# A mixture-of-experts guess computed in other steps and on VectorE alone, three query turns placed between exponentials, and expert weights loaded one matrix at a time

## The chip, the cores and the metric

The kernel runs on one NeuronCore of a Trainium2 chip. The metric is the device time of one execution in microseconds (us). The median of three runs of the kernel before is 532.5 us (531.18 to 532.99). The core has a matrix engine (TensorE, PE in the profile; its weight loads are PEld), VectorE (DVE), ScalarE (ACT), GpSimd (POOL), and SyncE (SP), which here only issues DMAs. Each engine works through its own instructions in the order in which the program lists them.

## What is computed

Attention with one shared key and value head per batch entry (8 entries, 16 query heads, 384 positions, head size 64), followed by a mixture of experts over 3072 tokens of width 1024: a group is picked by argmax of four logits, then an expert by argmax of four more, and the token goes through that expert's two 1024 x 1024 matrices.

```
scores = scale * q @ k.T ;  attn = softmax(scores) ;  attn_out = attn @ v
x = attn_out transposed and reshaped to (8*384, 16*64)
g_idx = argmax(x @ w_group) ;  g_w = softmax(...)[g_idx]
for each group g, each expert e of it:
    h = max(x_tokens @ w1[g, e], 0) ;  out[tokens] = g_w * e_w * (h @ w2[g, e])
```

## The kernel before, in words

**Tiling.** A batch entry (b) has three tiles of 128 queries, so there are 24 tiles (t). A tile has 8 units of two heads by 64 queries. The program is one long list of 96 steps (the loop over `i`, line 901), two units a step: four steps make a tile, twelve a batch entry. `at(step, place, function)` puts an action at a named place of a step, and `run(i, place)` calls it there; this fixes the order of each engine's instructions when the program is written. Nothing is reordered later.

**A step** does, in program order: the score matmuls of its first unit (L206, place "u" behind them), those of its second unit (place "s"), then `soft` (L212): a row maximum on VectorE for each unit (L217) and two exponentials on ScalarE for each unit (L220), with place "b" between the two units. Then come places "m0", "m1", "m3" with pieces of the expert's matmuls (`advance`), places "p", "v" and "m2", the 32 x 32 block transposes of the units of two steps ago on VectorE into a three-part buffer called `ring` (L241), place "w", the reciprocal of the sums on VectorE (L231) and the four normalising multiplications on GpSimd (L235), and places "e", "o" and "g".

**Scores** go to one of two PSUM buffers in turn, so the scores of a unit wait until the exponentials of the unit two before have been read out. The value matmuls (L257, `pv`) of a tile run two to four steps after the tile's last scores. For the first five tiles the queries are turned on TensorE (`q_group`, L174: four transposes, L183, into PSUM, then a copy on ScalarE, L187): each tile in two halves of eight heads. The second half of tile t is turned in step 4t, or 4t+1 where t is 1, 2 or 3, and is first used by the scores of step 4t+2; the first half of tile t+1 is turned in step 4t+1 and used from step 4t+4. Later tiles are turned on VectorE (`q_blocks`, L195). The load of tile t+2's queries (`load_q`, SP) stands at place "g" of the step that turns the last of tile t, whose buffer it takes.

**The guess.** Before any token's real gate is known, the kernel guesses one expert for each batch entry, so that this expert's weights can be loaded early. It adds up all value rows (`guess_load`, a 768 KB load on SP, and `guess_sum`, four additions on GpSimd, L360 and L361), forms their mean on TensorE (`guess_mean`, L370), its gate logits on TensorE (`guess_logits`, L382), picks the expert in one-hot form with seven small operations, four on VectorE and three on GpSimd (`guess_pick`, L389 to L413), spreads the result to all partitions on TensorE (`guess_all`, L419) and turns it into index numbers (`guess_index`, one operation on GpSimd, two on VectorE). All of it uses parts of `ring` that are not needed before step 6. What guess picks wrongly is handled by a loop at the end.

**Weights.** `load_main(b, 0)` and `load_main(b, 1)` load the first and second matrix of entry b's expert, each with two DMAs of 1024 KB (as landed, in bf16) issued by GpSimd (`load_w`, L536). There are two buffers of each matrix. The expert of entry b (`main_expert`, L561 for the first matrix, L575 for the second) starts on TensorE in step 12(b+1)+5 and is spread over twelve steps; it reads the first matrix for about seven of them, then the second. The expert of entry 0 therefore starts in step 17. `scale_k` (GpSimd, L167) and `k_blocks` (VectorE, L171) prepare the next entry's keys in steps 12b+7 and 12b+8.

Of the kernel before, what the change touches and what calls it, by code (L numbers as in the profile page):

```python
# [14 lines left out]
ALU = mybir.AluOpType  # L15
# [4 lines left out]
def kernel(  # L20
# [81 lines left out]
    def load_q(t, first=False):  # L102
        b, j = t // ST, t % ST
        q_sb = qpool.tile([P, 2 * H * D], FP32, tag="q", bufs=2)
        if t < TQ:
            q_sb = q_sb[:, 0:H * D].rearrange("p (h d) -> p h d", h=H)
            qv = q[b].rearrange("h (j r n) d -> j n r h d", n=QN, r=32)
            for h0 in range(0, H, H // 2 if first else H):
                for n in range(QN):
                    (nc.scalar if first and (n == 1 if h0 == 0 else n % 2) else nc.sync).dma_start(  # L110
                        out=q_sb[32 * n:32 * (n + 1), h0:h0 + (H // 2 if first else H), :],
                        in_=qv[j, n, :, h0:h0 + (H // 2 if first else H), :],
                    )
# [233 lines left out]
    def guess_load():  # L347
        vs = ring[:, 2, 0:2].rearrange("p u h s -> p (u h s)").rearrange("p (b c d) -> p b c d", b=B, d=D)
        nc.sync.dma_start(
            out=vs.rearrange("p b c d -> p b (c d)"), in_=v.rearrange("b o (p c) d -> p (b o) (c d)", c=ST)  # L350
        )
        st["vs"] = vs
# [36 lines left out]
    def guess_pick():  # L389

        lg = st["guess"]
        mx = [early[name][0:B] for name in ("mx", "sm")]
        oh = early["oh"][0:B].rearrange("b (g e) -> b g e", e=4)
        pair = early["pair"][0:B].rearrange("b (g e) -> b g e", e=Eg)
        spread = early["spread"][0:B].rearrange("b (c e) -> b c e", e=GE)
        gp = nc.gpsimd
        nc.vector.tensor_reduce(out=mx[0], in_=lg, axis=AX.X, op=ALU.max)
        gp.tensor_tensor(out=lg, in0=lg, in1=mx[0].unsqueeze(2).to_broadcast([B, 1 + G, 4]), op=ALU.subtract)
        nc.vector.scalar_tensor_tensor(
            out=lg, in0=lg, scalar=0.0, in1=w4[0:B, 0:1 + G, :], op0=ALU.is_ge, op1=ALU.mult  # L400
        )
        nc.vector.tensor_reduce(out=mx[1], in_=lg, axis=AX.X, op=ALU.max)
        nc.vector.tensor_tensor(
            out=oh, in0=lg, in1=mx[1].unsqueeze(2).to_broadcast([B, 1 + G, 4]), op=ALU.is_equal
        )
        gp.tensor_tensor(
            out=pair, in0=oh[:, 1:1 + G, :], in1=oh[:, 0, :].unsqueeze(2).to_broadcast([B, G, Eg]), op=ALU.mult
        )
        gp.tensor_tensor(
            out=spread, in0=pair.rearrange("b g e -> b (g e)").unsqueeze(1).to_broadcast([B, B, GE]),  # L410
            in1=ident[0:B, 0:B].unsqueeze(2).to_broadcast([B, B, GE]), op=ALU.mult,
        )
        st["guess"] = spread  # L413
# [10 lines left out]
            st["ohs", b] = [ohs_all[:, ts(b, GE)]]  # L424

    def guess_index():
        nc.gpsimd.tensor_tensor(
            out=numbered, in0=ohs_all[:].rearrange("p (b e) -> p b e", e=GE),
            in1=tie16[:].unsqueeze(1).to_broadcast([P, B, GE]), op=ALU.mult,
        )  # L430
        number = early["number"]
        nc.vector.tensor_reduce(out=number, in_=numbered, axis=AX.X, op=ALU.add)
        idx = singles.tile([P, B], I32)
        nc.vector.tensor_scalar(
            out=idx[:], in0=number, scalar1=-1.0, scalar2=float(GE - 1), op0=ALU.mult, op1=ALU.add
        )
        st["idx"] = idx
# [365 lines left out]
    def at(slot, where, fn, *args):  # L803
        later.setdefault((slot, where), []).append((fn, args))
# [6 lines left out]


    for x, where, fn in (
        (2, "e", guess_sum), (3, "m2", guess_mean), (4, "m2", guess_logits), (4, "e", guess_pick),
        (5, "m2", guess_all), (5, "e", guess_index),
    ):
        at(x, where, fn)
    for b in range(B):
        s0 = SB * b
        for x, j0, j1 in ((s0 + 8, 0, 1), (s0 + 16, 1, ST)) if b == B - 1 else ((s0 + 16, 0, ST),):  # L820
            at(x, "m2", logits, b, j0, j1)
            at(x + 1, "m0" if j1 < ST else "v", logits_out, b, j0, j1)
        if b == B - 1:
            at(s0 + 9, "m0", gate_first, b)
            at(s0 + 9, "m3", gate_choose, b)
            at(s0 + 9, "w", gate_score, b)
            at(s0 + 10, "w", gate_pick_second, b)
            at(s0 + 1, "g", load_main, b, 0)
            at(s0 + 6, "g", load_main, b, 1)
            at(s0 + 11, "g", load_second, 0)  # L830
        else:
            at(s0 + (9 if b else 7), "g", load_main, b, 0)
            at(s0 + (9 if b else 7), "g", load_main, b, 1)
            at(s0 + 16, "g", keep_xb, b)
        at(s0 + 17, "v", gate_masks, b)
        x = s0 + 18
        at(x, "e", gate_values, b)
        at(s0 + (19 if b == B - 2 else 22), "w", gate_selected, b)
        if b + 1 < B:
            at(s0 + 2, "g", load_k, b + 1)  # L840
            at(s0 + 4, "g", load_v, b + 1)
            at(s0 + 7, "g", scale_k, b + 1)
            at(s0 + 8, "e", k_blocks, b + 1)
    for t in range(NT):
        spread = 0 < t <= ST
        for x, u, half in ((4 * t + spread, t, 1), (4 * t + 1, t + 1, 0)):
            if u < TQ:
                at(x, "m1", q_group, u, half)
            elif u < NT:
                at(x, "e", q_blocks, u, half)  # L850
        if t < NT - 2:
            at(4 * t + spread, "g", load_q, t + 2)
        x, n0 = 4 * t + 4, 0
        for p, where, n1 in (
            ((2, "p", 4), (3, "u", 6), (3, "p", 8), (4, "u", 10), (4, "p", NB)) if t < ST - 1 else
            ((2, "p", NB // 2), (3, "p", NB)) if t < NT - 1 else ()
        ):
            at(x + p, where, pv, t, n0, n1)
            n0 = n1
            if n1 == NB:  # L860
                at(x + p, "o", pv_out, t)

    load_k_first()
    load_q(0, first=True)
    load_q(1)


    wge = singles.tile([P, KO, 32], FP32)
# [28 lines left out]
    busy(1)  # L897
    q_group(0, 0, 2)
    load_v(0)
    guess_load()  # L900
    for i in range(NSL):
        t, p = i // 4, i % 4
        if i >= SB + 5 and (i - 5) % SB == 0:
# [162 lines left out]
```

## Time and profile before

| what | value |
|---|---|
| time of the profiled execution | 530.77 us |
| its span in the profile | 529.3 us |
| three timed runs | 532.5, 531.18, 532.99 us |
| mean granted TensorE clock | 0.966 |
| weights: DMA issues, size, median time to landing | 36 of 1024 KB, 15.2 us |
| HBM read, written | 102.30 MB, 19.40 MB |

The profile comes from one execution. A row of the timeline has the start (us from the span's start), the duration, the engine, the program line, the operation, what it writes and reads and how often; in brackets stands how long the engine had been idle before it, and behind the arrow what ended that wait. A row of a table by stage has the stretch, its length, the busy time and the number of instructions of each engine, the granted clock of TensorE (1.00 is full speed), the mean share of the DMA engines that were at work, and GB/s. TensorE's busy time counts cold matmuls at their longer duration, so a busy TensorE is not one at full speed.

### The profile page before, as it was taken

How to read it: one execution, taken by the hardware profiler on the slowest of the kernel's cores; microseconds unless marked ns; L12 is line 12 of the kernel's file. 1: busy time of each engine (PE TensorE's matmuls, PEld its weight loads, DVE VectorE, ACT ScalarE, POOL GpSimd, SP SyncE). 2: the span in 40 equal slices, each digit the busy share in tenths (PEclk: the TensorE clock that was granted, in tenths of full speed). 3: DMA queues.
4: the chain of work that ended last, by engine and by line, in shares of the span. 5: the costliest groups of instructions: out<-in, count | busy, mean ns of one | idle time of the engine just before them, and what ended most of it. 6: DMA issues, size and time to landing. Idle time of an engine off the chain costs nothing.

```text
span 529.3 us, 19245 instructions
## 1 busy us (share of the span) xinstructions
PE 496.1 (94%) x7868; PEld 264.3 (50%) x7868; DVE 405.0 (77%) x678; ACT 322.6 (61%) x1005; POOL 293.5 (55%) x532
## 2 busy tenths in 40 slices
PE   6569569999999999999999999999999999999994
PEld 3224225555545545554555554554555455555653
DVE  3558686998879887898789887898699888890540
ACT  4445464677666675667667666667667776663421
POOL 2744663578447655576537844765547663754300
PEclk9868798999999999999999999999999999999998
DMA  7720992638983899649982899379973999629953
GB/s 115 166 42 2 189 210 62 160 66 159 235 243 73 150 224 239 159 78 207 259 225 57 159 229 259 72 137 218 231 185 74 200 238 279 125 50 180 220 121 108
DMA packets 65561, 84.78 MB, mean 160 GB/s; under 512 B 20395, under 2 KB 41003, under 8 KB 65472
## 3 DMA queue, kind: packets, MB, share of 16 engines
q0 software_dynamic: 19152, 37.84, 39.7%
q1 hardware_dynamic: 45360, 45.40, 34.4%
q8 instruction: 63, 1.03, 0.8%
q10 hardware_dynamic: 960, 0.30, 0.2%
q14 instruction: 26, 0.21, 0.1%
HBM read 102.30 MB, written 19.40 MB: 230 GB/s over the span
## 4 chain that ended last, share of the span: by engine, by line
PE 86%; DMA 4%; DVE 3%; ACT 2%; POOL 2%; issue 1%; SPq 0%; POOLq 0%; DVEq 0%; ACTq 0%
PE x L257 24%; PE s L206 24%; PE x L561 14%; PE x L575 12%; DMA q_sb<-in_q_dram 4%; PE sb L575 4%; ACT pr L220 2%; PE sb L561 2%; PE x L280 2%; DVE nmx L217 2%; DVE ring L241 1%; POOL pr L235 1%; PE x L756 1%; PE x L100 1%; PE x L771 0%
## 5 line engine op out<-in xcount | busy, mean ns | idle before, releaser
L235 POOL TENSOR_SCALAR pr<-pr,rinv 128x384 f32<-128x384 f32 x384 | 218.3, 588 | 166.1 <-DVE rinv L231 148.6
L220 ACT ACTIVATE pr<-s,nmx 128x384 f32<-128x384 f32 x384 | 218.1, 579 | 148.1 <-DVE nmx L217 117.4
L217 DVE TENSOR_REDUCE nmx<-s 128x2 f32<-128x768 f32 x192 | 174.9, 949 | 67.9 <-PE s L206 67.1
L241 DVE STREAM_TRANSPOSE ring<-pr 128x768 f32<-128x768 f32 x192 | 175.2, 951 | 0.6 <-PE x L257 0.6
L206 PE MATMUL s<-kt,qt 64*64 64x384 f32 x1536 | 154.9, 515 | 14.2 <-ACT qt L187 8.1
L257 PE MATMUL x<-ring,v_sb 32*64 32x256 f32 x4608 | 144.7, 385 | 1.3 <-issue 1.0
L257 PEld LDWEIGHTS x<-ring,v_sb 32*64 32x64 f32 x4608 | 101.4, 133 | 53.6 <-issue 33.1
L206 PEld LDWEIGHTS s<-kt,qt 64*64 64x64 f32 x1536 | 49.7, 136 | 84.5 <-ACT pr L220 31.5
L220 ACT ACTIVATION_READ_ACCUMULATOR pr<-s,nmx 128x1 f32 x384 | 77.7, 202 | 0.0
L561 PE MATMUL x<-xb,w 128*128 128x384 bf16 x448 | 76.5, 326 | 0.0
L561 PEld LDWEIGHTS <-w 128*128 128x128 bf16 x512 | 48.1, 98 | 42.5 <-issue 12.6
L575 PE MATMUL x<-w,h_t 128*128 128x512 bf16 x288 | 65.3, 380 | 0.0
L575 PEld LDWEIGHTS <-h_t 128*128 128x128 bf16 x384 | 35.7, 98 | 52.0 <-issue 11.9
L271 ACT COPY xt<-x 128x256 f32<-128x256 f32 x96 | 29.1, 387 | 4.2 <-PE x L257 4.1
L536 POOL DMA_DIRECT2D w<-in_moe_w_dram x36 | 27.8, 779 | 3.2 <-PE sb L575 2.4
L272 POOL CAST xb<-xt 128x1024 bf16<-128x1024 f32 x24 | 24.9, 1038 | 6.0 <-ACT xt L271 6.0
L567 ACT ACTIVATE h_t<-x 128x384 bf16<-128x384 f32 x56 | 24.7, 503 | 3.8 <-PE x L561 3.8
L593 ACT ACTIVATE y<-x,gsel 128x512 f32<-128x512 f32 x36 | 25.0, 693 | 3.3 <-PE x L575 3.3
L195 DVE STREAM_TRANSPOSE qt<-q_sb 128x512 f32<-128x512 f32 x38 | 26.1, 687 | 0.0
L575 PE MATMUL sb<-w,h_t 128*128 128x512 bf16 x96 | 21.5, 379 | 0.0
L593 ACT ACTIVATE y<-sb,gsel 128x512 f32<-128x512 f32 x9 | 6.2, 687 | 16.6 <-PE sb L575 16.6
L231 DVE RECIPROCAL rinv<-ssum 128x4 f32<-128x4 f32 x96 | 13.5, 140 | 3.2 <-ACT pr L220 3.2
(154 smaller groups left out, 161.0 us busy)
## 6 DMA issues: line engine op xcount, KB each, us to landing
w<-in_moe_w_dram POOLq DMA_DIRECT2D x36, 1024.0 KB, 15.2
q_sb<-in_q_dram SPq DMA_DIRECT2D x76, 224.0 KB, 5.4
out_dram<-y SPq DMA_DIRECT2D x96, 128.0 KB, 5.9
xb_scratch<-xb SPq DMA_DIRECT2D x8, 768.0 KB, 4.5
v_sb<-in_v_dram SPq DMA_DIRECT2D x32, 96.0 KB, 3.5
kk<-in_k_dram SPq DMA_DIRECT2D x28, 92.0 KB, 4.0
q_sb<-in_q_dram SPq DMA_DIRECT2D x16, 128.0 KB, 5.2
ring<-in_v_dram SPq DMA_DIRECT2D x1, 768.0 KB, 5.8
```

Source lines behind the costliest of these rows:

```text
L195: nc.vector.transpose(out=qt[:].rearrange("p (x d) -> p x d", d=32), in_=q_sb[:, :, 0:32])
L206: nc.tensor.matmul(out=s[m * D:(m + 1) * D, h, 0:S], lhsT=qt[r, ts(2 * cc + m, D)], rhs=kt[r, :], start=True, stop=True, tile_position=(h ...
L217: nc.vector.tensor_reduce(out=nmx[:], in_=s[:, :, 0:S], axis=AX.X, op=ALU.max, negate=True)
L220: nc.scalar.activation(out=pr[:, h, :], in_=s[:, h, 0:S], func=ACTF.Exp, bias=nmx[:, h:h + 1], scale=1.0, accum_out=ssum[:, k, h:h + 1],)
L235: nc.gpsimd.tensor_scalar(out=pr, in0=pr, scalar1=rinv[:, k, h:h + 1], scalar2=1.0, op0=ALU.mult, op1=ALU.mult)
L241: nc.vector.transpose(out=ring[:, (u // 4) % 3, u % 4].rearrange("p h s -> p (h s)"), in_=st.pop(("pr", u))[:].rearrange("p h s -> p (h s)"),)
L257: nc.tensor.matmul(out=o[i][h * D:(h + 1) * D, 0:2 * P].rearrange("d (g c q) -> d g c q", g=2, c=4), lhsT=v_sb[r, n, :], rhs=ring[r, a:z + ...
L271: nc.scalar.copy(out=xt[:, :, ts(i, 32)], in_=o[:, 0:2 * P].rearrange("p (c q) -> p c q", c=KO))
L536: nc.gpsimd.dma_start(out=w[:, o:o + 4, :], in_=(w1f, w2f)[n][ds(e, 1), :, o:o + 4, :].rearrange("o p c f -> (o p) c f"))
L561: nc.tensor.matmul(out=hp[:, 0:S], lhsT=w1[:, ko, ts(fc, P)], rhs=xb[:, ko, :], start=(ko == 0), stop=(ko == KO - 1))
L575: nc.tensor.matmul(out=yp, lhsT=h_t[:, fo, ts(j, P)], rhs=w2[:, fo, ts(nh, 512)], start=(fo == 0), stop=(fo == FO - 1),)
L593: nc.scalar.activation(out=y[:, ts(nh, 512)], in_=yp, func=ACTF.Copy, scale=g)
```

## The change

Three things change.

- The load for the guess is issued on SP right behind the first two query loads, ahead of the five small loads of the gate weights and of the first values. The guess's parts move: the sum from step 2 to step 1 (place "e"), the mean from step 3 to 2 and the logits from 4 to 3 (both "m2"), the pick from place "e" of step 4 (behind the reciprocal and the multiplications) to place "w" of step 4 (ahead of them), the index from place "e" of step 5 to "w" of step 6. All operations of the pick and of the index now run on VectorE; the four additions of the sum stay on GpSimd.
- For tiles 1, 2 and 3, the second half is turned at place "b" of steps 5, 9 and 13, between the exponentials of the step's two units, and no longer at "m1" behind all four.
- The two matrices of an expert are loaded in different steps: for entry 0 in steps 10 and 15 (both in step 7 before), for entries 1 to 6 in steps 12b+7 and 12b+11 (both in 12b+9 before), for entry 7 in steps 87 and 91 (85 and 90 before).

```diff
-        gp = nc.gpsimd
         nc.vector.tensor_reduce(out=mx[0], in_=lg, axis=AX.X, op=ALU.max)
-        gp.tensor_tensor(out=lg, in0=lg, in1=mx[0].unsqueeze(2).to_broadcast([B, 1 + G, 4]), op=ALU.subtract)
+        nc.vector.tensor_tensor(out=lg, in0=lg, in1=mx[0].unsqueeze(2).to_broadcast([B, 1 + G, 4]), op=ALU.subtract)
...
-        gp.tensor_tensor(
+        nc.vector.tensor_tensor(
             out=pair, in0=oh[:, 1:1 + G, :], in1=oh[:, 0, :].unsqueeze(2).to_broadcast([B, G, Eg]), op=ALU.mult
         )
-        gp.tensor_tensor(
+        nc.vector.tensor_tensor(
             out=spread, in0=pair.rearrange("b g e -> b (g e)").unsqueeze(1).to_broadcast([B, B, GE]),
...
     def guess_index():
-        nc.gpsimd.tensor_tensor(
+        nc.vector.tensor_tensor(
             out=numbered, in0=ohs_all[:].rearrange("p (b e) -> p b e", e=GE),
...
-        (2, "e", guess_sum), (3, "m2", guess_mean), (4, "m2", guess_logits), (4, "e", guess_pick),
-        (5, "m2", guess_all), (5, "e", guess_index),
+        (1, "e", guess_sum), (2, "m2", guess_mean), (3, "m2", guess_logits), (4, "w", guess_pick),
+        (5, "m2", guess_all), (6, "w", guess_index),
...
-            at(s0 + 1, "g", load_main, b, 0)
-            at(s0 + 6, "g", load_main, b, 1)
+            at(s0 + 3, "g", load_main, b, 0)
+            at(s0 + 7, "g", load_main, b, 1)
             at(s0 + 11, "g", load_second, 0)
         else:
-            at(s0 + (9 if b else 7), "g", load_main, b, 0)
-            at(s0 + (9 if b else 7), "g", load_main, b, 1)
+            at(s0 + (7 if b else 10), "g", load_main, b, 0)
+            at(s0 + (11 if b else 15), "g", load_main, b, 1)
...
             if u < TQ:
-                at(x, "m1", q_group, u, half)
+                at(x, "b" if half and spread else "m1", q_group, u, half)
...
     load_q(1)
+    guess_load()
...
     load_v(0)
-    guess_load()
```

More of the change, by code (lines that the diff above doesn't have):

```diff
@@ L395, in guess_pick @@
         spread = early["spread"][0:B].rearrange("b (c e) -> b c e", e=GE)
-        gp = nc.gpsimd
         nc.vector.tensor_reduce(out=mx[0], in_=lg, axis=AX.X, op=ALU.max)
-        gp.tensor_tensor(out=lg, in0=lg, in1=mx[0].unsqueeze(2).to_broadcast([B, 1 + G, 4]), op=ALU.subtract)
+        nc.vector.tensor_tensor(
+            out=lg, in0=lg, in1=mx[0].unsqueeze(2).to_broadcast([B, 1 + G, 4]), op=ALU.subtract
+        )
         nc.vector.scalar_tensor_tensor(
@@ L426, in guess_index @@
     def guess_index():
-        nc.gpsimd.tensor_tensor(
+        nc.vector.tensor_tensor(
             out=numbered, in0=ohs_all[:].rearrange("p (b e) -> p b e", e=GE),
```

## The prediction

> **What bounds the kernel now.** I read the page first, then the table by stage.
>
> ```profile
> span 529.3 us, 19245 instructions
> ...
> PE 496.1 (94%) x7868; PEld 264.3 (50%) x7868; DVE 405.0 (77%) x678; ACT 322.6 (61%) x1005; POOL 293.5 (55%) x532
> ...
> PEclk9868798999999999999999999999999999999998
> ```
>
> ```profile
> 20.00:38.00 18.00, 11.11 (x98) 5.77 (x102) 9.45 (x17) 7.62 (x27) 9.65 (x18) 0.67 0.29 69
> ...
> 155.00:480.00 325.00, 324.49 (x5403) 174.34 (x5409) 278.34 (x439) 218.45 (x689) 200.24 (x354) 1.00 0.80 172
> ```
>
> From 155 to 480 us TensorE is busy for 324.49 of 325 us at clock 1.00: every wait of another engine there is covered, and only less matmul work would shorten it. Nothing in the change removes matmuls. Before about 96 us it is otherwise: TensorE has gaps and runs below full speed, at 0.67 from 20 to 38 us. So the change is worth what it does to the time at which entry 0's expert starts (step 17). The starts of the score matmuls, the rows of the first unit of steps 2 to 17, without step 12's, in order, show where that time is:
>
> ```profile
> 13.27 0.88 PE L206 MATMUL s<-kt,qt 64*64 64x384 f32 x8 [0.86 <-ACT pr L220]
> ...
> 16.72 0.88 PE L206 MATMUL s<-kt,qt 64*64 64x384 f32 x8 [1.45 <-ACT pr L220]
> ...
> 24.45 2.84 PE L206 MATMUL s<-kt,qt 64*64 64x384 f32 x16
> ...
> 28.42 2.84 PE L206 MATMUL s<-kt,qt 64*64 64x384 f32 x16 [0.50 <-ACT pr L220]
> ...
> 37.15 2.84 PE L206 MATMUL s<-kt,qt 64*64 64x384 f32 x16 [2.60 <-ACT qt L187]
> ...
> 43.44 0.88 PE L206 MATMUL s<-kt,qt 64*64 64x384 f32 x8
> ...
> 47.15 0.88 PE L206 MATMUL s<-kt,qt 64*64 64x384 f32 x8
> ...
> 51.22 0.88 PE L206 MATMUL s<-kt,qt 64*64 64x384 f32 x8 [0.29 <-ACT pr L220]
> ...
> 59.55 2.84 PE L206 MATMUL s<-kt,qt 64*64 64x384 f32 x16 [5.30 <-ACT qt L187]
> ...
> 64.89 0.88 PE L206 MATMUL s<-kt,qt 64*64 64x384 f32 x8
> ...
> 72.67 0.88 PE L206 MATMUL s<-kt,qt 64*64 64x384 f32 x8 [0.30 <-ACT pr L220]
> ...
> 80.31 2.84 PE L206 MATMUL s<-kt,qt 64*64 64x384 f32 x16
> ...
> 86.37 1.52 PE L206 MATMUL s<-kt,qt 64*64 64x384 f32 x16
> ...
> 90.60 1.52 PE L206 MATMUL s<-kt,qt 64*64 64x384 f32 x16
> ...
> 94.16 0.88 PE L206 MATMUL s<-kt,qt 64*64 64x384 f32 x8
> ```
>
> Call the distance from one step's start to the next its pitch. An undisturbed step takes 3.45 us without value matmuls (step 2), 3.71 with half a tile's share (step 7), 4.23 where a full half tile's value matmuls run (step 15). Five steps stand out: 3 (7.73), 5 (8.73), 6 (6.29), 9 (8.33) and 13 (7.64). Each of them, except step 6, leaves TensorE idle, and the next matmuls then run at half clock: sixteen score instructions take 2.84 us there and 1.52 at 86.37.
>
> **The change part by part.** The rows behind the stalls, from the timeline, and two of the page's DMA list (the load for the guess, the early query loads; the last number is the median time to landing):
>
> ```profile
> 6.24 0.42 SPq L870 DMA_DIRECT2D wge<-in_moe_w_group_dram  x1
> ...
> 14.65 2.27 POOL L235 TENSOR_SCALAR pr<-pr,rinv 128x384 f32<-128x384 f32 x4 [1.16 <-DVE rinv L231]
> ...
> 22.72 0.72 POOL L361 TENSOR_TENSOR ring<-ring 128x256 f32<-128x256 f32 x1
> ...
> 23.50 1.02 PE L370 MATMUL x<-ident,ring 128*64 128x1 f32 x16 [0.85 <-POOL ring L361]
> ...
> 30.04 0.13 DVE L397 TENSOR_REDUCE ring<-ring 8x5 f32<-8x20 f32 x1
> ...
> 32.70 0.17 DVE L399 SCALAR_TENSOR_TENSOR ring<-ring,w 8x20 f32<-8x20 f32 x1 [2.53 <-POOL ring L398]
> ...
> 33.19 1.80 DVE L217 TENSOR_REDUCE nmx<-s 128x2 f32<-128x768 f32 x2
> ...
> 35.39 0.58 ACT L220 ACTIVATE pr<-s,nmx 128x384 f32<-128x384 f32 x1
> ...
> 36.52 1.07 ACT L187 COPY qt<-x 128x512 f32<-128x512 f32 x2
> ...
> 39.66 0.29 DVE L432 TENSOR_REDUCE ring<-ring 128x8 f32<-128x128 f32 x1 [2.83 <-POOL ring L427]
> ```
>
> ```profile
> q_sb<-in_q_dram SPq DMA_DIRECT2D x16, 128.0 KB, 5.2
> ...
> ring<-in_v_dram SPq DMA_DIRECT2D x1, 768.0 KB, 5.8
> ```
>
> Sum and mean: no gain. The four additions stay on GpSimd and the mean stays one step behind them, so TensorE, which works in order, now waits ahead of step 3's scores. The value load takes the place of 6.24 on SP, so with 5.8 it lands at about 12 and is not what GpSimd waits for. Step 1's multiplications end at 14.65 + 2.27 = 16.92, four additions of 0.72 end at 19.9, and the second half of the mean's matmuls needs 1.0 more (23.44 to 24.45 today): step 3 starts at 20.9, 4.2 later than today. Step 3's own pitch falls from 7.73 to step 4's 3.97, which is also half clock: 3.8 back. Net loss 0.4. Next in line are the logits: their copy of the mean finds ScalarE empty, and the gate weights and first values, 0.4 later on SP, are needed in steps 3 and 6.
>
> Pick. VectorE today goes from 30.04 to 33.19 with the pick, 3.15 us, because its second operation waits for GpSimd's, queued behind step 4's multiplications. From 32.70 to 33.19 three of the small ones follow each other, 0.16 each; at 0.2 the seven on VectorE are 1.4: 1.75 off step 5's pitch. Bounds for the seven: 1.1 (0.16 each) and 2.0 (0.29 each, the 128 x 128 row). Queued behind it now are step 4's reciprocal and multiplications, first needed by the transposes of step 6: covered.
>
> Turn between exponentials. Step 6's scores wait for a copy (2.60 idle) that stands behind all four exponentials; the second unit's two run from 35.39 to 36.52. Moved ahead of them, the copy comes 1.13 earlier in steps 5 and 9. The added wait on ScalarE, the transposes on TensorE, is over by then (they follow the scores at once). Queued behind the copy are the second unit's exponentials, 0.6 later; the next step's second scores wait for them, which follow 0.6 behind the first anyway at full speed. I take 1.13; bounds 0 and 1.13. So step 5 becomes 8.73 - 1.75 - 1.13 = 5.85: 2.9 gained.
>
> Step 6 lost its time to half-clock score and value matmuls and to VectorE's 2.83 wait for the numbering on GpSimd. With step 5's gap down from 2.6 to about 1 us I take the pitch of step 7, 3.71: 2.6 gained. The index now costs VectorE about 0.3 + 0.29 + 0.17 (the 128 x 128 reduction's 0.29 as the nearest row for the new operation), 0.75 on step 7's start of maxima: 0.75 lost.
>
> ```profile
> 51.31 3.25 POOL L536 DMA_DIRECT2D w<-in_moe_w_dram x4
> ...
> 55.14 0.58 DVE L171 STREAM_TRANSPOSE kt<-kk 128x384 f32<-128x384 f32 x1 [2.06 <-POOL kk L167]
> ...
> 79.30 1.08 PE L183 MATMUL x<-ident,q_sb 128*128 128x128 f32 x4 [4.04 <-DMA q_sb<-in_q_dram]
> ...
> 96.09 4.07 PE L561 MATMUL x<-xb,w 128*128 128x384 bf16 x24
> ```
>
> ```profile
> 55.48 23.58 DMA q_sb<-in_q_dram
> ```
>
> Weights. Four issues hold GpSimd for 3.25 us ahead of `scale_k`, and VectorE's key transpose waits 2.06 for that in step 8. The move takes the wait out: step 9's pitch 8.33 - 2.06 - 1.13 (turn) = 5.14, 3.2 gained; step 10, at half clock today, goes from 5.34 to 3.71, 1.6 gained. The queries of tile 4 (issued at 55.48) share the DMA engines with these 4 MB and take 23.58 us; TensorE waits 4.04 for them in step 13. In the new order they go out at step 9, the first matrix one step later and behind its multiplications, so they should land in the page's 5.2, long before step 13. Step 13 becomes 3.45 + 0.6 (the copy) = 4.05, 3.6 gained; step 14, half clock today, 6.06 to 4.23, 1.8 gained. Behind the issues on GpSimd, 1.6 us in each of steps 10 and 15, stand the multiplications of steps 11 and 16, read two steps later. The later entries' moves lie under the full TensorE of 155 to 480 us: nothing; without that cover 1.6 per issue pair.
>
> Sum: -0.4 + 2.9 + 2.6 - 0.75 + 3.2 + 1.6 + 3.6 + 1.8 = 14.55. Entry 0's expert starts at 96.09 - 14.55 = 81.5. The profiled execution's own time is 530.77 (span 529.3 and 1.5 around it): 516.2. It lies 1.7 under the median of the runs, 532.5: from that, **517.9 us**, which I predict.
>
> **The rivals.** (1) The clock stays low. The stall ahead of step 3 is as long as today's ahead of step 4, so the clock should fall again. How long?
>
> ```profile
> 23.00:32.00 9.00, 8.00 (x68) 3.73 (x69) 3.77 (x6) 2.68 (x10) 4.49 (x9) 0.50 0.04 12
> ...
> 33.00:36.00 3.00, 0.63 (x3) 0.29 (x2) 2.96 (x6) 1.78 (x7) 0.60 (x2) 1.00 0.84 173
> ```
>
> For over 9 us, although TensorE was busy for 8.00 of 9. My sum has step 4 at today's half-clock pitch and full speed from step 6's value matmuls on. If it is low until their end, as until 43 us now, step 6 gains nothing (2.6) and the slow transposes and scores of step 5 eat the turn's gain there (1.1): 3.7 less, 521.6. Against it: TensorE is dense from the mean at 19.9 through step 3's scores and the logits, 4.6 us. [...]
>
> (2) The turn does not pay: the second unit's exponentials, 0.6 later, set the next step instead. For it: in step 4 one buffer's readout is what scores wait for (0.50 idle). Then 1.13 twice and 0.6 in step 13 fall away: 2.9 less, 520.8.
>
> (3) The collision moves. If the queries of tile 4 or 5 are still in flight when a matrix is issued in step 10 or 15, TensorE waits in step 13 or VectorE in step 17 as it does now: 4.04 of idle and the half clock behind it (3.6 + 1.8 of the sum at most): 523.3. Against it: step 9's issue has a whole step's lead, and one matrix is half the bytes.
>
> (4) Slower than before: the first matrix comes late. Today it is issued at 51.3 and needed at 96.1. In the new order it is issued behind step 10's multiplications, about 58, and needed at 81.5.
>
> ```profile
> DMA to landing us min/median/max: 7.9/15.2/26.6
> ```
>
> (All 36 weight issues.) At the median it is there at 75; at the worst, 85 with its second half, 4 us are lost, 521.8. Each further microsecond costs one, and from a landing at 96.1, 38 us after the issue, the kernel is slower than before; at twice the worst landing it would be there at 111, 29.5 late: 547. Nothing in the trace takes so long.
>
> (5) The change does not do what it says, in that the guess costs as much as today: then the pick and step 6 give nothing: 1.75 + 2.6 = 4.4 less, 522.3. Against: no GpSimd operation is left between VectorE's.
>
> **How the numbers follow.** Forecast 0.60, rival 1 0.14, rival 2 0.08, rival 3 0.06, rival 4 0.02 as a loss, rival 5 0.03. The remaining 0.07 is a larger gain: a stall ahead of step 3 that leaves the clock up gives 0.5 in each of steps 3 and 4, 516.9, and if the 1.7 between profile and median goes too, 515.2 and less. The range 514 to 523 takes in the bounds of pick and turn, rivals 1, 2 and 5, and leaves out rival 3, rival 4 and the far end of the larger gain, about 0.1. Faster by over 0.3% (about what a measurement of this kernel can tell from no change) 0.97, within it 0.01, slower 0.02: every rival but the fourth stays over 9 us below 532.5.
>
> **What would show it.** Right: the expert's first matmul (now L562) near 81.5 us; TensorE idle for some 3 us ahead of step 3's scores, behind GpSimd's additions; no GpSimd wait on VectorE in steps 4 to 8; steps 5, 9 and 13 with pitches of 5.9, 5.1 and 4.1; queries of tile 4 landing in under 8 us. Wrong: a wait of L562 on the weights, a DMA wait on L183, clock 0.50 beyond step 6, or any gap of TensorE after the expert's start, where my sum has none.

## The result, and the profile after

The changed kernel takes 525.56 us (median of 4 runs, 525.04 to 526.80), the kernel before 532.75 in the same session (531.18 to 534.17): a ratio of 0.9869, 95% interval 0.9835 to 0.9903. It is 7.2 us faster. The forecast was 517.9, a gain of 14.6 with a range of 514 to 523: the sign was right, half of the gain is missing, and the time lies outside the range.

The page of the changed kernel: its span, TensorE's busy time, the granted clock in 40 slices, the DMA queue that carries instructions and the later query loads (the last number is the median time to landing in us).

```profile
span 525.4 us, 19232 instructions
...
PE 495.2 (94%) x7851; PEld 264.3 (50%) x7868; DVE 405.6 (77%) x682; ACT 322.7 (61%) x1005; POOL 292.5 (56%) x528
...
PEclk9779899999999999999999999999999999999998
...
q8 instruction: 63, 1.03, 0.8%
...
q_sb<-in_q_dram SPq DMA_DIRECT2D x76, 224.0 KB, 11.3
```

The busy time of TensorE is that of before to a microsecond; the clock dips in three slices instead of five; the later queries land in 11.3 us at the median instead of 5.4. What changed is where TensorE is idle. First the front. The timeline of TensorE in the changed kernel, with the score matmuls at which steps 3, 4, 5, 6, 9, 10, 11, 13, 14 and 15 begin, and the expert's first matmul:

```profile
18.34 0.63 PE L370 MATMUL x<-ident,ring 128*64 128x1 f32 x16 [3.19 <-POOL ring L361]
...
20.78 2.83 PE L206 MATMUL s<-kt,qt 64*64 64x384 f32 x16
...
24.75 2.84 PE L206 MATMUL s<-kt,qt 64*64 64x384 f32 x16 [0.50 <-ACT pr L220]
28.71 2.84 PE L206 MATMUL s<-kt,qt 64*64 64x384 f32 x16 [1.13 <-ACT pr L220]
...
34.50 0.88 PE L206 MATMUL s<-kt,qt 64*64 64x384 f32 x8 [0.91 <-ACT qt L187]
...
46.15 0.88 PE L206 MATMUL s<-kt,qt 64*64 64x384 f32 x8
...
51.39 0.88 PE L206 MATMUL s<-kt,qt 64*64 64x384 f32 x8 [2.06 <-ACT qt L187]
...
53.36 3.57 PE L257 MATMUL x<-ring,v_sb 32*64 32x256 f32 x64
56.86 0.88 PE L206 MATMUL s<-kt,qt 64*64 64x384 f32 x8
...
64.64 0.88 PE L206 MATMUL s<-kt,qt 64*64 64x384 f32 x8 [0.30 <-ACT pr L220]
...
69.20 0.88 PE L206 MATMUL s<-kt,qt 64*64 64x384 f32 x8 [1.54 <-ACT qt L187]
...
73.92 1.52 PE L206 MATMUL s<-kt,qt 64*64 64x384 f32 x16
...
83.65 4.07 PE L562 MATMUL x<-xb,w 128*128 128x384 bf16 x24
```

The front went nearly as forecast. The wait for GpSimd's additions stands ahead of step 3 (3.19 us), step 3 starts at 20.78 (forecast 20.9), step 5's pitch is 34.50 - 28.71 = 5.79 (5.85), step 9's 5.24 (5.14), and the 4.04 us wait for tile 4's queries is gone. Entry 0's expert starts at 83.65 instead of 96.09: 12.44 us gained, where the sum had 14.55.

From there on the lead is lost again. In before 529.3 - 96.09 = 433.2 us lie between the expert's first matmul and the end, in the changed kernel 525.4 - 83.65 = 441.75. The table by stage, at the stretch that the prediction called full (the first numbers are its length and TensorE's busy time; in before the latter was 324.49):

```profile
155.00:480.00 325.00, 319.60 (x5221) 171.12 (x5241) 266.87 (x418) 211.34 (x664) 195.46 (x347) 1.00 0.79 168
```

TensorE is now idle for 5.4 us of a stretch in which the sum had nothing, at clock 1.00. The waits of TensorE from 97 to 500 us (total, times, longest), first before:

```profile
PE x L257 <- issue: 1.0, 3, 0.5
```

and after:

```profile
PE x L257 <- issue: 5.2, 8, 1.0
PE s L206 <- DVE ring L241: 0.3, 1, 0.3
```

No engine and no semaphore released these waits: "issue" is time in which the engine waited for nothing that the profile shows, and all of it stands ahead of the value matmuls. One of the eight, after, in the second half of the value matmuls of step 35:

```profile
166.12 2.88 PE L257 MATMUL x<-ring,v_sb 32*64 32x256 f32 x96
168.93 1.52 PE L206 MATMUL s<-kt,qt 64*64 64x384 f32 x16
170.38 1.94 PE L257 MATMUL x<-ring,v_sb 32*64 32x256 f32 x52
173.28 1.54 PE L257 MATMUL x<-ring,v_sb 32*64 32x256 f32 x44 [0.96 <-issue]
```

The same group in before:

```profile
181.53 2.85 PE L257 MATMUL x<-ring,v_sb 32*64 32x256 f32 x96
```

A full group of 96 takes 2.85 us. This one stops after 52 matmuls, and the pieces on both sides of the gap are long too: 4.44 us from its start to its end, 1.59 over 2.85. I call this the group's excess. Over all groups after the expert's start (those with over 0.15 us of it) it is 13.1 us in the changed kernel and 5.1 in the first profile of before; 0.5 more stand ahead of the expert there. The difference, 8.0, is most of the 8.55 lost.

### The profile page after: what moved, and what is told of

Same layout as the page of the kernel before. It is cut to its first block, busy times and chain, and to the rows that moved or that the text cites. A ratio compares the mean times of both kernels' runs of the same rounds, so it can differ in the third digit from the quotient of the medians.

```text
span 525.4 us, 19232 instructions
## 1 busy us (share of the span) xinstructions
PE 495.2 (94%) x7851; PEld 264.3 (50%) x7868; DVE 405.6 (77%) x682; ACT 322.7 (61%) x1005; POOL 292.5 (56%) x528
## 3 DMA queue, kind: packets, MB, share of 16 engines
q8 instruction: 63, 1.03, 0.8%
## 4 chain that ended last, share of the span: by engine, by line
PE 87%; DVE 4%; ACT 3%; issue 3%; POOL 2%; POOLq 0%; DVEq 0%; ACTq 0%
PE x L257 25%; PE s L206 24%; PE x L562 14%; PE x L576 12%; PE sb L576 4%; ACT pr L220 3%; PE sb L562 2%; PE x L280 2%; DVE nmx L217 2%; DVE ring L241 2%; POOL pr L235 1%; PE x L757 1%; PE x L100 1%; PE x L772 0%; PE x L183 0%
## 5 line engine op out<-in xcount | busy, mean ns | idle before, releaser
L206 PE MATMUL s<-kt,qt 64*64 64x384 f32 x1536 | 152.8, 508 | 11.3 <-ACT pr L220 6.2
L257 PE MATMUL x<-ring,v_sb 32*64 32x256 f32 x4608 | 147.7, 383 | 5.2 <-issue 5.2
L257 PEld LDWEIGHTS x<-ring,v_sb 32*64 32x64 f32 x4608 | 102.9, 132 | 57.2 <-issue 35.0
L206 PEld LDWEIGHTS s<-kt,qt 64*64 64x64 f32 x1536 | 48.5, 134 | 82.5 <-ACT pr L220 36.2
## 6 DMA issues: line engine op xcount, KB each, us to landing
q_sb<-in_q_dram SPq DMA_DIRECT2D x76, 224.0 KB, 11.3
```

The source lines that it names most:

```text
L206: nc.tensor.matmul(out=s[m * D:(m + 1) * D, h, 0:S], lhsT=qt[r, ts(2 * cc + m, D)], rhs=kt[r, :], start=True, stop=True, tile_position=(h ...
L257: nc.tensor.matmul(out=o[i][h * D:(h + 1) * D, 0:2 * P].rearrange("d (g c q) -> d g c q", g=2, c=4), lhsT=v_sb[r, n, :], rhs=ring[r, a:z + ...
```

## What stops TensorE: two theories

**Theory F (fetch).** By it, TensorE's own instructions are a transfer, and TensorE stops in the middle of a group where the next packet is late. The page has 63 packets with 1.03 MB in the instruction queue q8, 16 KB each, and TensorE ran 7868 matmuls and as many weight loads: one packet is some 250 instructions, and its loaded instructions are called a block below. A group of 96 value matmuls uses up 192 instructions in 2.85 us, sixteen score matmuls 32 in 1.52. The page counts these packets on the same 16 DMA engines as weights and queries (0.8% of their time for q8). The DMA view of the changed kernel from 168 to 176 us (40 slices of 0.2 us, the group begins at 170.38):

```profile
DMA  9999999999999999999999999999997771000000
...
q8 instruction: 2, 0.03, 1.8%
```

and of before from 176 to 184 us, ahead of the same group at 181.53:

```profile
DMA  9999995400002000694924599999999999999999
...
q8 instruction: 1, 0.02, 0.7%
```

In the changed kernel the packet starts at 170.78, amid weights and queries, and ends at 171.74; the matmuls go on at 173.28, 1.5 us after it (1.4 and 1.3 at the gaps of steps 27 and 43). In before it starts at 178.50, in the gap between two loads, 3 us ahead of its group. The times of single packets are from the trace's DMA records.

**Rival S (shift).** The later steps of the guess and the turn on ScalarE stand otherwise against the rest, and the main stage pays for that whatever the weights do.

The places of the gaps say where the boundaries are. Counted through the traces of all fourteen profiles (two instructions for a weight load and its matmul, one for every other instruction of TensorE), all 91 gaps of TensorE from 40 to 500 us that are put down to "issue", most of them in value matmuls, eight in scores, one in the expert, stand at the same place of a run of 256 instructions, the 194th or 195th. That is what a stream loaded in blocks of 256 gives, and a wait for data would not.

The packets that matter are every fifth one: the eight gaps of the changed kernel stand 1280 instructions, five blocks, or 2560 apart. Every second tile has a packet boundary inside its second half of value matmuls: steps 27, 35, 43 ... 83. For these, worked out from the trace's records: how long after TensorE began the block ahead of the missing one the packet starts (negative: earlier), and the excess of the group, in us. Here the blocks are counted as multiples of 256 from the first record; counted from the place of the gaps, all starts are 0.8 to 1.4 us larger, and the two kinds stay apart: 0.4 to 0.8 without excess, 2.4 to 3.9 with it.

```
step of the group          27    35    43    51    59    67    75    83
before         start      2.1  -0.4   1.6   2.1  -0.3   1.5   1.9  -0.1
               excess     0.8   0     0.4   0.8   0     0.6   0.8   0
after          start      2.5   3.1   3.0   2.2   2.3   2.2   2.6   3.0
               excess     1.1   1.6   1.7   1.0   0.5   1.1   1.3   1.6
```

A start of -0.4 or so goes with a DMA share of at most 0.28 in the 1.5 us ahead of it, a start of 1.5 or more with a share of 1.04 to 1.16 (packets of several queues overlap in the records, so the share can pass 1). A full share is not enough by itself: in slots_split, below, the packets of steps 27, 59 and 83 start at 0.2 to 0.7 in the table's count with a share of 1.07 to 1.12, and their groups have no excess. In before, with both matrices in one step of twelve, three of the eight packets met free engines. With the matrices in two steps, none does.

## The experiments

Twelve kernels; each ratio is to runs of the kernel before on the same chip, with its 95% interval.

**late_w_old**: the changed kernel with the old weight steps for all entries but the first.

```
-            at(s0 + (7 if b else 10), "g", load_main, b, 0)
-            at(s0 + (11 if b else 15), "g", load_main, b, 1)
+            at(s0 + (9 if b else 10), "g", load_main, b, 0)
+            at(s0 + (9 if b else 15), "g", load_main, b, 1)
```

(and 1 and 6 instead of 3 and 7 for the last entry.)

> The changed kernel with the weights of entries 1 to 7 loaded in the steps of before (both matrices in step 12b+9; 85 and 90 for the last entry); entry 0 keeps steps 10 and 15, and everything else of the change stays. Theory F (fetch): TensorE's instructions come as packets of 16 KB over the same DMA engines as the weights; with the weights spread over more of the time more of these packets start late, and TensorE stands still inside the value matmuls (the rows 'PE x L257 <- issue'). Then the issue gaps fall back to about those of before: from the expert's first matmul (83.7 us) to the end 434 us instead of 441.75, and the time is about 518.5 us (517 to 520.5). Rival S: the lead is given back because the steps of the front and the turn on ScalarE stand otherwise against the rest, whatever the weights do: it stays at 525 to 526.

521.27 us, 0.9793 (0.9757 to 0.9830): 4.3 us below the changed kernel (4.0 by the two ratios, which takes out that they ran in two sessions), with the expert's first matmul at 83.65 as there. Rival S is out. The time is 0.8 above theory F's range: the excess falls from 13.1 only to 8.1. The groups of steps 35, 59 and 83 lose theirs (packets at -0.5, -0.5 and -0.1), and the other five keep it. TensorE's row from 155 to 480 us:

```profile
155.00:480.00 325.00, 322.09 (x5314) 172.30 (x5307) 266.98 (x416) 212.63 (x668) 195.38 (x348) 1.00 0.81 173
```

**late_w_new**: the kernel before with only the later entries' weights moved, 7 and 11 for 9 and 9, and 3 and 7 for 1 and 6 in the last entry.

> The kernel before, with the weights of entries 1 to 7 alone moved to the new steps (12b+7 and 12b+11; 87 and 91 for the last); entry 0's weights, the guess and the turn stay as before. Theory F: the expert's first matmul stays at 96 us, the long groups of value matmuls (5.6 us over 2.85 each in before) add up to 12 us or so, and the time is 537 to 540 us, slower than before. Rival S (the weights' steps do not matter once TensorE is full, which is what the prediction held): 532 to 533.5.

538.01 us, 1.0104 (1.0078 to 1.0129): this part alone makes the kernel before slower by 6.2 us (531.79 there). Excess 13.5; all eight packets late (1.8 to 3.1), as in the changed kernel. The two rows, waits of TensorE from 97 to 500 us and the stretch from 155 to 480:

```profile
PE x L257 <- issue: 6.3, 9, 1.1
```

```profile
155.00:480.00 325.00, 319.74 (x5306) 171.59 (x5311) 273.03 (x432) 214.12 (x679) 193.29 (x339) 1.00 0.80 171
```

319.74 with the old front and 319.60 with the new one: the loss belongs to the weights' steps and to nothing else in the change.

**half_block**: the changed kernel with half a packet of instructions more, early.

```
+    def pad(x):
+        for _ in range(64):
+            nc.tensor.matmul(out=x[:, 0:8], lhsT=blank[:, 0:P], rhs=blank[:, 0:8], start=True, stop=True)
+    at(2, "m2", lambda: pad(xbank()))
```

> The changed kernel with 64 matmuls of 8 columns on a zero tile ahead of the guess's mean in step 2, where TensorE waits 3.19 us: 128 more TensorE instructions, half of a 16 KB packet, so that every later packet boundary falls half a packet earlier against the steps. Theory F: the long groups of value matmuls leave the second halves of the tiles at steps 27, 35, 43, 51 ... and appear, if anywhere, at those of steps 31, 39, 47 ...; the time goes anywhere from 517 to 527 as these meet the transfers or not. Rival S, or any cause in the data that the value matmuls read (VectorE's ring, the values): the same groups stay long, and the time stays within 2 us of 525.5. The clock ahead of step 3 may stay higher by these matmuls, which is read apart, from the start of the expert.

529.54 us over all nine runs (529.1 without the longest, 534.48), 0.9942 (0.9912 to 0.9972), above what either theory gave. The expert starts late, at 87.37, but not by the 64 matmuls themselves: step 15 starts at 72.23, ahead of the 73.92 of the changed kernel. Its value matmuls then stop for a packet, the longest such gap of all, and the clock is at half speed from 77.70 to 84.53:

```profile
77.89 2.82 PE L257 MATMUL x<-ring,v_sb 32*64 32x256 f32 x34 [2.23 <-issue]
```

The places are what this run was for. The changed kernel's long groups at steps 27, 35, 43, 51, 59, 67 and 83 are 2.85 us here, and long are those of 31, 39, 47, 55, 63, 71, 79 and 87 (and of 15, 19, 23 and 75). The timeline of half_block around steps 31 to 35:

```profile
151.90 2.85 PE L257 MATMUL x<-ring,v_sb 32*64 32x256 f32 x96
...
156.13 1.12 PE L257 MATMUL x<-ring,v_sb 32*64 32x256 f32 x32
158.38 1.99 PE L257 MATMUL x<-ring,v_sb 32*64 32x256 f32 x64 [1.13 <-issue]
...
171.36 2.85 PE L257 MATMUL x<-ring,v_sb 32*64 32x256 f32 x96
...
175.59 2.85 PE L257 MATMUL x<-ring,v_sb 32*64 32x256 f32 x96
```

156.13 is step 31's second half and 175.59 step 35's. Step 35 has the same data, the same weights and the same steps as in the changed kernel; the count of instructions ahead of it differs, and with it the times of the front. The gaps of over 0.15 us stand again at the 194th or 195th instruction of a run of 256, now 128 instructions earlier in the program. So what the value matmuls read is not the cause; the packet boundary is.

**no_weights**: the changed kernel without the weights of entries 2 to 7.

```
-        st.setdefault(("w", b), []).append(load_w(st["e", b], n))
+        st["last", n] = st["last", n] if b > 1 else load_w(st["e", b], n)
+        st.setdefault(("w", b), []).append(st["last", n])
```

> The changed kernel without the weight loads of entries 2 to 7 (24 of the 36 transfers of 1 MB): their experts use the matrices of entry 1, so the output differs, and the work of TensorE is the same. Theory F: with the weights off the DMA engines the instruction packets start in time, the long groups of value matmuls are left only where the loads of keys, values and queries run (13.1 us of excess in all falls to 3 to 6), and the time is 516.5 to 520. Rival S, or packets that are slow whatever the engines carry: the excess stays over 10 us and the time at 524 to 526.

517.78 us, 0.9728 (0.9702 to 0.9754), as theory F had it. That it is almost the forecast's 517.9 is in part luck: the expert starts at 83.60 here, 2.1 later than the forecast's 81.5, and the forecast had added 1.7 for the base. Excess 5.0; left are steps 19 and 27 (0.6 and 1.1, beside the weights of entry 1, still loaded), steps 43 and 67 (1.2 and 1.1, beside other loads) and one near the end (0.9). It takes the issues off GpSimd too, so by itself it does not tell these from the transfers; slots_split below keeps every issue and loses the same groups.

```profile
155.00:480.00 325.00, 322.93 (x5382) 173.94 (x5388) 268.10 (x422) 213.43 (x670) 179.00 (x326) 1.00 0.41 98
```

**slots**: weights only behind the steps with a packet boundary.

```
+            at((10, 19, 27, 43, 51, 67, 75)[b], "g", load_main, b, 0)
+            at((15, 27, 35, 51, 59, 75, 83)[b], "g", load_main, b, 1)
```

> The changed kernel with the weights of entries 1 to 6 issued only in steps 19, 27, 35, 43, 51, 59, 67, 75 and 83 (the first matrix of entries 1 to 6 in 19, 27, 43, 51, 67, 75, the second in 27, 35, 51, 59, 75, 83), right behind the steps in which the long groups of value matmuls stand, so that the transfers are over when the next of these comes eight steps later; entry 0 and the last entry as in the changed kernel. Theory F: the long groups lose most of their excess, 13.1 us in all to 5 or less, and the time is 516.5 to 519.5. Rival S: 525 to 526.

537.49 us, 1.0099 (1.0065 to 1.0134): a clear miss. The packets were late less often (0.6 us of issue gaps ahead of value matmuls; the excess of 7.3 is in part half clock), but steps 27, 51 and 75 issue 4 MB ahead of a query load. VectorE's waits, 84 to 520 us:

```profile
DVE qt L195 <- DMA q_sb<-in_q_dram: 16.3, 3, 5.7
```

what the first of them does on VectorE:

```profile
170.69 0.71 DVE L195 STREAM_TRANSPOSE qt<-q_sb 128x512 f32<-128x512 f32 x1 [5.70 <-DMA q_sb<-in_q_dram]
```

and on TensorE:

```profile
173.62 2.84 PE L206 MATMUL s<-kt,qt 64*64 64x384 f32 x16 [3.99 <-ACT pr L220]
```

TensorE waits 3.99, 3.81 and 3.31 us, and each time the scores behind it run at half clock (2.84 for 1.52). It is the collision of the prediction's rival 3 at another place.

**slots_early**: the same a step earlier (18, 26, 42, 50, 66, 74 and 26, 34, 50, 58, 74, 82; last entry 84 and 90).

> Like slots, with every issue one step earlier (first matrices in 18, 26, 42, 50, 66, 74; second in 26, 34, 50, 58, 74, 82; last entry 84 and 90), so that the transfers begin right behind the long groups of value matmuls and the queries loaded two steps later have a step more to land. Theory F: the queries' wait (5.7 us on VectorE, three times in slots) goes or falls below 1 us, the long groups stay at 5 us or less of excess in all, and the time is 516 to 519.5. If the queries' transfers are behind 4 MB of weights all the same: 525 to 537.

521.12 us, 0.9789 (0.9765 to 0.9813), between the two ranges. Excess 3.9: steps 27, 35, 51, 59, 75 and 83 are clean. The query waits shrink but do not go:

```profile
DVE qt L195 <- DMA q_sb<-in_q_dram: 4.8, 3, 1.9
```

The profiled execution also lost 2.5 us ahead of the expert (86.17), in code that it shares with the changed kernel: a 1.81 us issue gap amid step 14's scores. A packet can be late in the front too.

**slots_split**: the first matrices of entries 2, 4 and 6 three steps later (29, 53, 77).

> Like slots_early, with the first matrix of entries 2, 4 and 6 three steps behind the second matrix of the entry before it (29, 53 and 77 instead of 26, 50 and 74), so that the queries loaded in steps 28, 52 and 76 meet 2 MB instead of 4. Theory F: the three waits of VectorE for queries (4.8 us in all) go, the excess of the long groups stays near 4 us, and the time is 516.5 to 519.5. If the second matrix then meets the packet of the next long group (step 34), the gaps come back there: 520 to 523.

519.48 us (517.15 to 520.18), 0.9749 (0.9716 to 0.9783): at the upper end of theory F's range and the fastest of the kernels that do the whole work, 6 us below the changed one. VectorE's waits for queries are gone. Excess 4.5; steps 43 and 67 keep theirs (1.5 and 1.2), beside keys, values and queries. Its waits on TensorE from 90 to 500 us, the second half of step 35, and the stretch from 155 to 480:

```profile
PE x L257 <- issue: 1.9, 3, 0.9
PE s L206 <- ACT xt L271: 1.8, 1, 1.8
PE x L576 <- DVE nmx L217: 0.6, 1, 0.6
```

```profile
170.33 2.85 PE L257 MATMUL x<-ring,v_sb 32*64 32x256 f32 x96
```

```profile
155.00:480.00 325.00, 322.40 (x5372) 174.02 (x5385) 267.05 (x416) 212.65 (x666) 193.54 (x345) 1.00 0.81 173
```

**slots_split_v**: also the values and the token matrix's copy four steps later (`load_v` at `s0 + 8`, `keep_xb` at `s0 + 20`).

> Like slots_split, with the values of the next entry and the copy of the token matrix to memory four steps later (12b+8 instead of 12b+4), off the long groups that stand at steps 43, 67 and 91. Theory F: the excess there (1.48, 0.97 and 0.96 us in slots_early) falls too, and the time is 0.5 to 2 us below that of slots_split. Against: the later transfers meet another group, and the time is the same or up to 3 us more.

523.97 us, 0.9854 (0.9828 to 0.9879): 4.5 us worse instead of better, and worse than the 3 us that the case against it allowed. Step 43's excess goes as intended, but step 31 gets an issue gap of 1.7 us, step 19 one of 0.97, and packets are now late in scores as well. Waits from 90 to 500 us:

```profile
PE x L257 <- issue: 3.2, 3, 1.7
PE s L206 <- issue: 1.5, 3, 0.7
```

Why that gap, at 157.15, is longer than any other behind the expert's start was not followed up.

**no_turn**, **old_guess**, **w0_old**: the changed kernel with one part of the front undone each, read at the expert's first matmul (83.65). Each is read from one profile. Seven profiles share the changed front up to the expert (the changed kernel, late_w_old, no_weights, slots, slots_early, slots_split, slots_split_v), and there this matmul stands at 82.70 to 86.17, four times within 0.1 of 83.65. So a difference of a microsecond or two in it is not told from chance; the pitches of steps 5, 9 and 13, which agree in the seven to 0.4, 0.2 and 0.0, are surer.

```
-                at(x, "b" if half and spread else "m1", q_group, u, half)
+                at(x, "m1", q_group, u, half)
```

> The changed kernel with the turn of the second half of the queries back where it was, behind all four exponentials. To be read at the expert's first matmul (83.65 us in the changed kernel), which the later packets cannot touch. By the sum of the prediction (1.13 in steps 5 and 9, 0.6 in step 13) it comes 2.9 us later, at 86.5. Rival 2 (the turn does not pay): it stays at 83.7.

85.34, and 527.49 us, 0.9915 (0.9889 to 0.9942): 1.7 later at the expert, not 2.9, and within the spread above. The turn's direct gain is there, 6.95 - 5.79 = 1.16 in step 5, 0.91 in step 9, 1.12 in step 13; what is missing is the clock: step 10 is at full speed here and at half speed in the changed kernel (see the last section).

For old_guess the four `nc.vector.tensor_tensor` go back to `nc.gpsimd` and the steps to:

```
+        (2, "e", guess_sum), (3, "m2", guess_mean), (4, "m2", guess_logits), (4, "e", guess_pick),
+        (5, "m2", guess_all), (5, "e", guess_index),
```

> The changed kernel with the guess as before: four of its operations on GpSimd, its steps 2 to 5 instead of 1 to 6, its load behind the first values. By the sum (pick 1.75, step 6 2.6, index -0.75, sum and mean -0.4) the expert's first matmul comes 3.2 us later, at 86.9. Rival 5 (the guess costs as much on VectorE): within 0.5 of 83.7. If the clock ahead of step 4 rather than the guess made step 6 slow, about 85.5.

88.71, and 531.85 us, 0.9993 (0.9975 to 1.0011). 5.1 us later, 0.65 of it an issue gap at 79.71: the guess is worth 4.4 by this profile, where the sum had 3.2; the 1.2 between them are not told from chance. Rival 5 is out: 88.71 lies beyond all seven.

```
+            at(s0 + 7, "g", load_main, b, 0)
+            at(s0 + (11 if b else 7), "g", load_main, b, 1)
```

> The changed kernel with both matrices of entry 0 issued in step 7, as before; the rest of the change stays. By the sum (wait of the key transpose 2.06, the queries' stall in step 13 without the copy's 0.6 3.0, its half clock behind it 1.8; step 10's 1.6 did not come) the expert's first matmul is 6.9 us later, at 90.5. Rival: the other gains of the front bring the queries' due time nearer to the same transfer, and it costs more: 91.5 to 93.

90.85, and 534.29 us, 1.0044 (1.0018 to 1.0069): 7.2 us later (6.9 expected; to be read with the same spread). Without the new steps of entry 0's weights the change as a whole is slower than the kernel before.

**before_again**: how much of the full stage is chance.

> The kernel before, unchanged, profiled a second time, to see how much of the full stage is chance. The first profile (span 529.3) was among its quickest executions, with TensorE busy for 324.49 of 325 us from 155 to 480 us. If the wait for instruction packets differs from execution to execution, this one shows 322 to 323.5 us there and a time of 531.5 to 533; then the 2.4 us that the changed kernel with the old weight steps lacks in that stage (322.09) need no cause of their own. If the stage is the same to 0.3 us in every execution, it shows 324.2 to 324.5, and those 2.4 us come from the earlier front.

532.51 us (one run, beside 531.98), 322.11 us busy from 155 to 480, excess 7.3:

```profile
155.00:480.00 325.00, 322.11 (x5334) 173.34 (x5343) 278.08 (x438) 217.52 (x688) 198.29 (x346) 1.00 0.79 172
```

The packet of step 43 starts 2.8 us late here and 1.6 in the first profile, and 1.4 us of excess stand where there were 0.4; the three packets between the loads are at -0.4, -0.3 and -0.1 in both. So the first profile of before was a lucky one, and late_w_old's 322.09 agrees with this profile of the old front: it needs no second cause.

## Why the prediction was wrong, point by point

- **The step that failed**: "The later entries' moves lie under the full TensorE of 155 to 480 us: nothing". TensorE's busy time covers the waits of the other engines, and I took it to cover everything. It does not cover TensorE's own instruction packets, at whose boundaries the 5.2 us of issue gaps stand. The moves cost 4.3 us with the new front (525.56 against 521.27; 4.0 by the ratios) and 6.2 with the old one (538.01 against 531.79). The prediction named a gap of TensorE after the expert's start as what would prove it wrong, and that is what came, but it was no rival with a price. A second of its signs came too, clock 0.50 beyond step 6 (in step 10, see below).
- **Where it could be seen**: the profile of before already had three issue gaps in the value matmuls (145.24, 452.44 and 486.12) and the q8 row. I read 324.49 of 325 as "full" and did not ask what the missing half microsecond was.
- **Step 10's clock, 1.6**: did not come in this profile. Step 10's pitch is 5.47 instead of 3.71, its value matmuls from 53.36 at half clock. Of the seven profiles with this front, three (late_w_old, slots_split, slots_split_v) have 3.85 or 3.86 there, at full clock: whether this term came went with where the stretches of the last section lie, and the sum had it as certain. Steps 13 and 14, 4.56 and 4.72 instead of 4.05 and 4.23, lack another 1.0, in all seven. Against these 2.8 us stand 0.75 that the sum had taken off for the index and that were not lost: steps 7 and 8 take 3.93 and 3.86, together 0.75 less than it had. That leaves the 2.1 us by which the expert came later than the sum; the other terms held (step 3 at 20.78; pitches 5.79, 3.86 and 5.24 in steps 5, 6 and 9).
- **A reading of the clock that was too coarse**: rival 1 took the 9 us at half clock with TensorE busy for 8.00 of them as one stretch. Cut into stretches of 3.41 us (last section) from the fall of the clock at 22.76, TensorE is busy there for 2.67, 2.92 and 3.41 us, and full speed comes back right behind the third. In the changed kernel, from the fall at 19.11, it is 2.70, 2.91, 2.29 and 3.41, and full speed comes back behind the fourth, at 32.77: the 4.6 us of dense work that rival 1 had against it did not bring it back earlier. Not to count on an early return was right all the same: step 4's pitch is 3.97.
- **The turn**: the mechanism was right (1.16, 0.91 and 1.12 against 1.13, 1.13 and 0.6); it then meets the clock. Rival 2, that it does not pay, is out.
- **The guess and entry 0's weights**: 4.4 and 7.2 by undoing each, against 3.2 and 6.9.
- **The base**: I moved from the profiled 530.77 to the median 532.5 as if the 1.7 were a constant. The two profiles of this kernel put it down to the packets' luck: 322.11 against 324.49 us busy in the same stretch, 2.4 us.
- **The account**: in the two other executions of the old front the expert starts at 95.30 and 95.52 (before_again, late_w_new), so the front gains about 11.8, 2.8 less than the sum. Less the 4.0 to 4.3 for the later moves, 7.5 to 7.8 remain; measured were 7.2.

## What to carry to other kernels

A TensorE that was busy for 99.8% of a stage (324.49 of 325 us) still depended on the DMA engines for its instructions here: with the weights moved it was idle for 5.4 us of that stage. Where many small matmuls run (30 ns each here), look for "issue" gaps in their rows and for the instruction queue's packets, and ask of every moved load which packet it will meet. Spreading a load thinner over time was worse here than one burst (538.01 us against 531.79), as it left no free stretch for the packets that matter. Loads behind the groups that cross a packet boundary gave 519.48 us where they were clear of the next load's due time (slots_split) and 537.49 where they were not (slots). Before a span is used as a base, profile the kernel twice: the two of before are 529.3 and 531.1 us.

## What the runs showed of the hardware that was not expected

- A late packet cost TensorE 0.4 to 1.7 us at a time in the groups of the table (2.3 in step 31 of slots_split_v; 4.2 in step 15 of half_block, half clock included), and where it struck moved with the instruction count ahead of it: 128 more instructions moved the stalls by four steps. Packets take 0.9 to 1.5 us each in the records (0.96 both for the one amid weights and queries at 170.78 and for the one between two loads at 178.50 in before); what differs is when they start. What holds them back was not measured.
- The clock did not follow the length of the stall. The table by stage for step 10, in no_turn with a wait of 3.12 us ahead of it, and in the changed kernel with one of 2.06 (the clock is the number ahead of the last two):

```profile
54.57:57.93 3.36, 3.36 (x81) 1.86 (x81) 2.42 (x3) 1.80 (x6) 2.04 (x4) 1.00 0.09 17
```

```profile
51.39:56.86 5.47, 5.21 (x80) 2.37 (x81) 4.47 (x7) 3.92 (x13) 2.99 (x6) 0.69 0.28 48
```

  In the clock records of the front the stretches at half clock are whole multiples of 3.41 us: 13.65 and 3.41 in the changed kernel, 13.65 and 3.41 in no_turn, 6.83 and 3.41 in slots_split, whose front is that of the changed kernel. So the traces are cut here into stretches of 3.41 us, laid out from the edges in each profile's own clock records.

  The falls of the clock go with TensorE's busy time in such a stretch. The least busy ones around the wait ahead of step 10, in the changed kernel, no_turn and slots_split (behind the stretch's length stands TensorE's busy time):

```profile
49.83:53.25 3.42, 1.60 (x16) 0.42 (x16) 3.05 (x5) 3.12 (x10) 2.22 (x4) 1.00 0.80 158
```

```profile
49.62:53.03 3.41, 1.83 (x16) 0.99 (x16) 3.41 (x6) 2.31 (x9) 2.65 (x5) 1.00 0.23 54
```

```profile
47.58:50.99 3.41, 1.78 (x16) 0.95 (x16) 3.41 (x6) 2.25 (x9) 2.64 (x5) 1.00 0.26 59
```

  Behind the first, with 1.60 us busy, the clock falls; behind the other two, with 1.83 and 1.78, it stays at 1.00. In the fourteen profiles, from about 10 to 510 us, it falls behind 40 of these stretches; TensorE was busy for 0 to 1.72 us of 3.41 in 39 of them and for 2.12 in one. It stays up behind none with less than 1.64. It comes back behind stretches with 2.91 to 3.41 us busy and stays down behind those with less and behind a few as busy. So the same wait went with a fall of the clock or not by where the edges of these stretches lay, and that differed between the profiles (49.83 and 47.58 above, with step 10's scores at 51.39 and 51.42): the waits of 1.99 to 2.06 us ahead of step 10 had a fall behind them in four of the seven profiles with this front. A sum should hold such a term as a range.
